# Chunk 5's LayerNorm statistics behind the last kv visit, and the last pair's second product in two column halves

## The chip, the core and the metric

One core of a Trainium2 chip runs the whole program. The metric is the device time of one execution in microseconds. The kernel before took 358.76 us as the median of 3 runs (358.67 to 359.09).

## What is computed

With `q`, `k`, `v` of shape 1 x 2048 x 448, the result is the sum of the input and of two branches on its LayerNorm (no scale, no shift):

```python
x = A_q
xn = _layernorm(x, axis=-1)
return x + _A_ref(xn, A_k, A_v, A_shift_k, A_ssm_k, A_ssm_D) + _B_ref(xn, B_w1, B_b1, B_w2)
```

`_A_ref` makes `kv` (a causal four-tap filter of `k` along the sequence, times `v`), convolves each of its 448 channels with a filter as long as the sequence (written in the reference as a product of FFTs), adds `kv * ssm_D`, and multiplies by `xn`. `_B_ref` is `mish(xn @ w1 + b1) @ w2` with a hidden width of 1792.

## The kernel before

**Two streams of work share every engine.** The dense branch goes through 8 chunks of 256 rows. A chunk is 7 pairs, and a pair is two blocks of 128 hidden columns. For each of the 56 pairs, `g1_mm` (line 514) makes the first product in 22 matmuls of 256 columns, `mish` (lines 522, 86, 87) takes the activation on ScalarE, rounds it to `ach` on ScalarE and makes the rest `acl` on VectorE, and two pairs later `g2_mm` (lines 546 to 548) adds the pair to the second product in 12 matmuls of 448 columns. Each float32 factor is the sum of a rounded part and a rest, so each product is three matmuls.

The long convolution is a Fourier transform in steps. `f1_mm` (line 148) makes the first step of the filter (visits "h") and of `kv` (visits "kv"), `f1_fold` (lines 154, 158) folds it on ScalarE and VectorE, and `f1_out` (line 169) writes it to the scratch tensors `Dh` and `Dkv`. Ahead of each of the 8 kv visits, `taps` (lines 191 to 204) makes `kv` on VectorE, with one tap on GpSimd (line 184). Then come 8 octaves: `hv_mm` (line 237) transforms both sides into `pp`, `pq` and `pr`, which are double-bank PSUM tiles, `h_out` (line 250) copies the filter's side to `hs` on ScalarE, `prod` (lines 259 to 266) multiplies on VectorE, and `i1_mm` (line 276) goes back. `i2_mm` (line 330) and `gate` finish it.

**What sets the order.** A loop over 116 slots, two for each pair, issues everything. Numbers at the head of the file say in which slot each step is issued. Each engine then works its own list strictly in that order. `g1_mm` of pair i stands in slot 2i, `mish` of pair i and `g2_mm` of pair i-2 in slot 2i+1. The last two kv visits are in slots 55 and 59, and the first octave's `hv_mm` is in slot 66.

**The statistics of a chunk.** For chunks 3 to 7, `nt_stats` queues five small VectorE steps on a list called `drip` (two of line 408, two of line 411, and one closure with line 414). `dv()` takes the next step off that list; calls of it are spread over the code, and `flush` takes all that is left. The last step also issues the power -0.5 on GpSimd (line 417) and, on GpSimd's queue, the store of mean and rstd to the scratch tensor `MR` (line 444). `nt_row` (line 447, SyncE's queue) loads one half of `MR` back, broadcast to all partitions, into the columns of `con` called `idr`, a single buffer. `nt_norm` (line 453) applies it to the transposed input `xn` with two VectorE operations. `nt_split` rounds the result to `XH` on ScalarE (line 460) and leaves the rest `XL` on VectorE (line 461). The table `NT_HOW` gives the slots of these steps relative to a base b, which is 56 for chunk 5. Chunk 5's first product starts in slot 70.

**In the first octave** the filter's two halves go to `pp` and `pq`, and the `kv` side's to `pr` and again to `pp`. So the fourth group of matmuls, into `pp`, has to wait until ScalarE's copy `hs<-pp` has read the first.

**The end.** After the last pair (chunk 7, pair 6), `g2_mm` runs for each half of 128 rows, followed by `g2_evac` (line 553, VectorE adds PSUM to `Q`) and a store of 224 KB on SyncE's queue (line 556).

Of the kernel before, what the change touches and what calls it, by code (L numbers as in the profile page):

```python
# [14 lines left out]
S, D, F = 2048, 448, 1792  # L15
NJ = 16
NF = F // 128
NP = NF // 2
CH = 256
NCHUNK = S // CH  # L20
# [13 lines left out]
NT_AT = {"q": -5, "x": -1, "stats": -2, "flush": 0, "row": (4, 8), "norm": (7, 10), "split": (8, 11)}  # L34
NT_SOON = dict(NT_AT, row=(4, 5), norm=(4, 7), split=(6, 8))
NT_HOW = {c: NT_SOON for c in (4, 7)}
NT_HOW[3] = dict(NT_SOON, q=-9, stats=-3, flush=-2)
NT_HOW[5] = dict(NT_AT, q=-8, stats=-4, flush=-2)
EVAC_SOON = 2,
WARM_N = (448, 448, 448)  # L40
FILL_N = (224, 112, 96)
# [3 lines left out]
def tile_kernel(ctx: ExitStack, tc, q, qT, k, v, sk, hT, sD, w10, w1, w2, c_fib, c_g, c_gi, c_i2, out):  # L45
    nc = tc.nc
    V = nc.vector
# [34 lines left out]
    w2h = wp.tile([128, NF, D], F32R, name="w2h")  # L82
    w2l = wp.tile([128, NF, D], F32R, name="w2l")
# [8 lines left out]
    def bank(n):  # L92
        return duo[n // 2][:, n % 2]
# [12 lines left out]
    def dv(n=1):  # L106
        for _ in range(n):
            if drip:
                drip.pop(0)()
# [182 lines left out]
    EE, QA, Q = {}, {}, {}  # L292
# [10 lines left out]
    def late(c):  # L303
        return c >= NCHUNK - LATE
# [84 lines left out]
    def ln_load(c, eng=None):  # L389
        Q[c] = mp.tile([128, 2, D], F32, name="qt", tag="qt", bufs=3)  # L390
        if c:
            nc.sync.dma_start(Q[c], q[:, 2 * c:2 * c + 2])
        else:
            for jj in range(2):
                nc.sync.dma_start(Q[c][:, jj], q[:, jj])
# [4 lines left out]
    def ln_parts(c):  # L400
        st = mp.tile([128, 2, 6], F32, name="bst", bufs=2)
        ve = mp.tile([128, 2], F32, name="ve", bufs=2)
        if c < NT:
            XN[c] = xn = xn_tile().rearrange("p a b -> p (a b)").rearrange("p (j d) -> p j d", j=2)
        eng = nc.gpsimd if 0 < c < NCHUNK - 1 else V

        def stats(jj):
            V.bn_stats(st[:, jj], Q[c][:, jj])

        def aggr(jj):  # L410
            V.bn_aggr(mv[:, 2 * c + jj], st[:, jj])

        def eps(a, b):
            V.tensor_scalar(ve[:, a:b], mv[:, 2 * c + a:2 * c + b, 1], EPS, None, op0=ALU.add)  # L414

        def power(a, b):
            nc.gpsimd.tensor_tensor(rs(c)[:, a:b], ve[:, a:b], mhalf[:, a:b], op=ALU.pow)  # L417

        def norm(jj):
            j = 2 * c + jj  # L420
            eng.tensor_scalar(xn[:, jj, :D], Q[c][:, jj], mv[:, j, 0:1], rs(c)[:, jj:jj + 1],
                              op0=ALU.subtract, op1=ALU.mult)

        def tail(a, b, copy=eng.tensor_copy):
            copy(xn[:, a:b, D:], xn[:, a:b, D - 64:D])

        return stats, aggr, eps, power, norm, tail, ve

    def ln_stats(c):
        stats, aggr, eps, power, norm, tail, ve = ln_parts(c)  # L430
        drip.extend([lambda: stats(0), lambda: stats(1), lambda: aggr(0), lambda: aggr(1), lambda: eps(0, 2),
                     lambda: [f(*a) for f, *a in ((power, 0, 2), (norm, 0), (tail, 0, 1), (norm, 1), (tail, 1, 2))]])
# [47 lines left out]
    def ln_T(c, jj):  # L480
        if jj == 0:
            dv(len(drip))
            x_tiles(c)
        p = pg()
        transposes(c, jj, p)
        for lo in range(2):
            x_split(c, jj, p, lo)


    AHL, P1, P2, GB = {}, {}, {}, {}  # L490
    held, hv = [], set()
    pairs = [(c, p) for c in range(NCHUNK) for p in range(NP)]

    def g1_mm(i):
        c, p = pairs[i]
        XH, XL = XS[c]
        pt = [(bank(GB[i]) if i in GB else pg()).rearrange("p (a b) -> p a b", a=2) for _ in range(2 if i == 0 else 1)]
        ps = [pt[n % len(pt)][:, n] for n in range(2)]
        mm = [[], []]
        for n in range(2):  # L500
            f = 2 * p + n
            fs = slice(128 * f, 128 * f + 128)
            hh, hl, lh = ([(w[:, kt, fs], x[:, kt]) for kt in range(3)] for w, x in ((w1h, XH), (w1h, XL), (w1l, XH)))
            th, tl = ((w1h[:, 3, fs], x[:, 3]) for x in (XH, XL))
            mm[n] = [(n, *m) for m in hh + lh + [th] + hl + [tl]]

            if 0 < i < NP:
                mm[n] = [(n, *m) for m in hh + hl + lh + [th, tl]]
        if i == 0:
            seq = mm[0][:7] + mm[1][:3] + mm[0][7:] + mm[1][7:10] + mm[1][3:7] + mm[1][10:]  # L510
        else:
            seq = mm[0] + mm[1]
        for n_, (n, l, r) in enumerate(seq):
            nc.tensor.matmul(ps[n], l, r, start=all(m[0] != n for m in seq[:n_]), stop=all(m[0] != n for m in seq[n_ + 1:]))  # L514
        P1[i] = ps

    def mish(i):
        p = pairs[i][1]
        ps = P1.pop(i)
        a = mp.tile([128, 2, CH], F32, name="a", bufs=2)  # L520
        for n in range(2):
            nc.scalar.activation(a[:, n], ps[n], AF.Mish, bias=b1t[:, 2 * p + n:2 * p + n + 1])  # L522
            if i == n == 0:
                w1_hi(2)
        if i == 0:
            w1_lo(2)
        ah = mp.tile([128, 2, CH], F32R, name="ach", bufs=3)
        al = mp.tile([128, 2, CH], F32R, name="acl", bufs=3)
        AHL[i] = ah, al
        if 2 * i + 1 in hv:  # L530
            held.append(lambda: split(ah, al, a))
        else:
            split(ah, al, a)
            dv()

    def g2_mm(i, jjs=(0, 1)):
        c, p = pairs[i]
        ah, al = AHL[i]
        for n in range(2):
            f = 2 * p + n  # L540
            for jj in jjs:
                if f == 0:
                    P2[c, jj] = g2p.tile([128, 512], F32, name="pg2")
                ps = P2[c, jj][:, :D]
                cs = slice(128 * jj, 128 * jj + 128)
                nc.tensor.matmul(ps, ah[:, n, cs], w2h[:, f], start=f == 0, stop=False)  # L546
                nc.tensor.matmul(ps, ah[:, n, cs], w2l[:, f], start=False, stop=False)  # L547
                nc.tensor.matmul(ps, al[:, n, cs], w2h[:, f], start=False, stop=f == NF - 1)  # L548

    def g2_evac(c, jjs=(0, 1)):  # L550
        x = Q[c]
        for jj in jjs:
            V.tensor_add(x[:, jj], P2.pop((c, jj))[:, :D], x[:, jj])
            dv()
            if late(c):
                nc.sync.dma_start(out[:, 2 * c + jj], x[:, jj])

    def g2_out(c):
        nc.sync.dma_start(out[:, 2 * c:2 * c + 2], Q[c])

    def mlp_slot(s):
        i, half = divmod(s, 2)
        n = len(pairs)
        j = i - G2_LAG
        if half == 0:
            if i < n:
                c, p = pairs[i]
                if c + 1 < NT:
                    if p == 0:
                        ln_load(c + 1)  # L570
                    if p == (3 if c in (0, 2) else 2):
                        ln_stats(c + 1)
                    if c == 0:
                        dv(len(drip))
                    if p == NP - 1:
                        ln_T(c + 1, 1)
                g1_mm(i)
        else:
            if i < n:
                c, p = pairs[i]  # L580
                if p == NP - 2 and c + 1 < NT:
                    ln_T(c + 1, 0)
                if s not in hv:
                    mish(i)
            if 0 <= j < n - 1:
                g2_mm(j)
                if pairs[j][1] == NP - 1 and pairs[j][0] in EVAC_SOON:
                    g2_evac(pairs[j][0])
            elif j == n - 1:
                for jj in range(2):  # L590
                    g2_mm(j, (jj,))
                    g2_evac(pairs[j][0], (jj,))


    ctx.enter_context(tc.manual_schedule())
# [76 lines left out]
    for c in range(NT, NCHUNK):  # L672
        at_ = NT_HOW.get(c, NT_AT)
        b = 2 * NP * (c - 1) + (1 if c < 5 else 0)
# [36 lines left out]
    stats, aggr, eps, power, norm, tail, ve = ln_parts(0)  # L711
# [5 lines left out]
    ps = [g2p.tile([128, 512], F32, name="pg2") for _ in range(2)]  # L717
# [29 lines left out]
    for s in range(nslots):  # L747
        j = s // 2 - G2_LAG - 1
        if s % 2 == 0 and j >= 0 and pairs[j][1] == NP - 1 and pairs[j][0] not in EVAC_SOON:
            g2_evac(pairs[j][0])  # L750
        if s in hv:
            mish(s // 2)
        for fn, args in plan.pop(s, ()):
            fn(*args)
        mlp_slot(s)
        fns = plan2.pop(s, ())
        for fn, args in fns:
            if fn is i1_out:
                fn(*args)
        for fn, args in fns:  # L760
            if fn is not i1_out:
                fn(*args)
# [69 lines left out]
```

## Time and profile before

| What | Value |
|---|---|
| Median of 3 runs | 358.76 us |
| Span of the profiled execution | 357.0 us (first to last instruction) |
| TensorE busy | 351.0 us, 98% |
| VectorE busy | 270.6 us, 76% |
| ScalarE busy | 156.6 us, 44% |
| GpSimd busy | 70.3 us, 20% |
| Mean granted TensorE clock | 0.998 |

The profiled execution has its span alone; its whole device time isn't listed. The median of the runs is 1.7 us longer than that span, and this stands for what lies around the span. Times in the rows are microseconds from the first instruction. PE is TensorE, PEld its weight loads, DVE VectorE, ACT ScalarE, POOL GpSimd and SP SyncE. In a row of the timeline the first number is the start, the second the duration (a merged row covers several instructions), and the brackets hold the engine's idle time before it and who ended that.

### The profile page before, as it was taken

To read this page: it belongs to the slowest core of one execution; us is meant where nothing else is said; L and a number is where in the kernel's file an instruction comes from. 1 tells how busy PE (TensorE), PEld (TensorE's weight loads), DVE (VectorE), ACT (ScalarE), POOL (GpSimd) and SP (SyncE) were. 2 spreads that over 40 slices of the span, in tenths; PEclk is the share of its full clock that TensorE was granted. 3 is DMA by queue.
4 is the path that set the end of the run, shared out by engine and by line. 5 is a ranking of instruction groups with operands and counts; after the bars stand their busy time and mean duration, and the time that the engine had idled before them with its cause. 6 is when DMAs were issued, how large, how long until landed. Compare 5 with 4: busy or idle time off the path is not lost.

```text
span 357.0 us, 7437 instructions
## 1 busy us (share of the span) xinstructions
PE 351.0 (98%) x3092; PEld 289.5 (81%) x3092; DVE 270.6 (76%) x375; ACT 156.6 (44%) x267; POOL 70.3 (20%) x78
## 2 busy tenths in 40 slices
PE   8999999999999999999999999999999999999995
PEld 2988888888888989888988757666775699979794
DVE  5989748999999999999437756756963933788941
ACT  4966552344243343343233454445445443354470
POOL 2037002822220240212000031011031116040030
PEclk9999999999999999999999999999999999999999
DMA  7998976949768637665869569999896387989086
GB/s 260 344 364 307 411 287 175 340 123 263 198 171 313 164 107 168 223 162 118 245 201 355 201 165 292 248 278 312 276 273 121 77 234 272 409 319 274 19 116 141
DMA packets 30691, 83.27 MB, mean 233 GB/s; under 512 B 3137, under 2 KB 15810, under 8 KB 30658
## 3 DMA queue, kind: packets, MB, share of 16 engines
q1 hardware_dynamic: 21842, 47.82, 39.4%
q0 software_dynamic: 4928, 22.95, 22.9%
q10 hardware_dynamic: 3888, 12.03, 12.8%
q8 instruction: 24, 0.39, 0.4%
q14 instruction: 9, 0.07, 0.1%
HBM read 54.34 MB, written 28.45 MB: 232 GB/s over the span
## 4 chain that ended last, share of the span: by engine, by line
PE 52%; issue 8%; DVE 6%; POOL 2%; DMA 1%
PE pq L514 7%; PE pg L546 7%; PE pg L548 7%; PE pg L547 6%; PE pp L514 5%; PE pr L514 4%; PE pp L237 3%; PE pr L237 3%; PE pp L276 2%; PE pg L514 2%; DVE x L201 2%; POOL x L184 2%; PE pq L237 2%; DMA xn<-in_qT_dram 1%; PE pr L276 1%
## 5 line engine op out<-in xcount | busy, mean ns | idle before, releaser
L546 PE MATMUL pg<-w2h,ach 128*128 128x448 f32 x224 | 82.5, 368 | 0.0
L548 PE MATMUL pg<-w2h,acl 128*128 128x448 f32 x224 | 81.4, 363 | 0.0
L547 PE MATMUL pg<-w2l,ach 128*128 128x448 f32 x224 | 81.2, 362 | 0.0
L87 DVE TENSOR_TENSOR acl<-a,ach 128x512 fp32r<-128x512 f32 x56 | 38.9, 695 | 31.7 <-ACT ach L86 31.5
L522 ACT ACTIVATE a<-pg,b1t 128x256 f32<-128x256 f32 x66 | 27.8, 472 | 65.4 <-PE pg L514 43.3
L514 PE MATMUL pg<-XH,w1h 128*128 128x256 f32 x264 | 52.6, 283 | 0.0
L546 PEld LDWEIGHTS pg<-w2h,ach 128*128 128x128 f32 x224 | 41.9, 187 | 11.5 <-issue 7.2
L514 PEld LDWEIGHTS pg<-XH,w1h 128*128 128x128 f32 x264 | 41.4, 188 | 6.9 <-issue 5.6
L547 PEld LDWEIGHTS pg<-w2l,ach 128*128 128x128 f32 x224 | 42.1, 188 | 2.4
L548 PEld LDWEIGHTS pg<-w2h,acl 128*128 128x128 f32 x224 | 42.1, 188 | 2.4
L514 PE MATMUL pg<-XL,w1h 128*128 128x256 f32 x264 | 42.9, 277 | 0.0
L158 DVE TENSOR_TENSOR st<-pq,st 128x896 f32<-128x896 f32 x32 | 34.8, 1089 | 4.8 <-ACT st L154 4.3
L514 PEld LDWEIGHTS pg<-XL,w1h 128*128 128x128 f32 x264 | 35.9, 188 | 0.0
L86 ACT CAST ach<-a 128x512 fp32r<-128x512 f32 x56 | 34.8, 622 | 1.7
L514 PE MATMUL pg<-XH,w1l 128*128 128x256 f32 x198 | 33.6, 278 | 0.0
L184 POOL TENSOR_TENSOR x<-kr,skb 128x896 f32<-128x896 f32 x8 | 17.0, 2123 | 70.9 <-PE pr L148 26.2
L514 PEld LDWEIGHTS pg<-XH,w1l 128*128 128x128 f32 x198 | 27.6, 188 | 0.2 <-DVE w1l L372 0.2
L201 DVE TENSOR_TENSOR x<-x 128x896 f32<-128x896 f32 x24 | 26.2, 1091 | 1.5 <-POOL x L184 0.8
L522 ACT ACTIVATE a<-pq,b1t 128x256 f32<-128x256 f32 x20 | 8.4, 471 | 31.8 <-PE pq L514 31.8
L287 POOL DMA_DIRECT2D E<-qe x14 | 8.7, 628 | 63.1 <-ACT qe L284 63.1
L154 ACT COPY st<-pr 128x896 f32<-128x896 f32 x16 | 14.5, 908 | 14.2 <-PE pr L148 12.3
L417 POOL TENSOR_TENSOR mv<-ve,mhalf 128x2 f32<-128x2 f32 x5 | 5.0, 1007 | 72.0 <-DVE ve L414 72.0
(138 smaller groups left out, 605.7 us busy)
## 6 DMA issues: line engine op xcount, KB each, us to landing
Dkv<-st ACTq DMA_DIRECT2D x16, 448.0 KB, 5.3
ah<-Dh SPq DMA_DIRECT2D x8, 896.0 KB, 7.5
av<-Dkv SPq DMA_DIRECT2D x8, 896.0 KB, 8.6
e<-E POOLq DMA_DIRECT2D x8, 896.0 KB, 7.2
E<-qe POOLq DMA_DIRECT2D x14, 448.0 KB, 5.9
kr<-in_k_dram SPq DMA_DIRECT2D x10, 448.0 KB, 6.8
Dh<-st ACTq DMA_DIRECT2D x10, 448.0 KB, 6.2
x<-in_hT_dram SPq DMA_DIRECT2D x8, 448.0 KB, 6.0
```

The source lines that it names most:

```text
L86: nc.scalar.copy(h, raw)
L87: V.tensor_sub(l, raw, h)
L154: nc.scalar.copy(st[:, 1], o)
L158: f(st[:, n], e, st[:, 1])
L184: nc.gpsimd.tensor_mul(o, KR[g - u // 2], skb[:, u:u + 1].to_broadcast([128, 2, D]))
L201: V.tensor_add(KV[g], KV[g], o)
L237: nc.tensor.matmul(p[32 * t:32 * t + 32, r, :D], g[rs, t, c], a[rs, t], start=True, stop=True, tile_position=(64 * r, 32 * t))
L514: nc.tensor.matmul(ps[n], l, r, start=all(m[0] != n for m in seq[:n_]), stop=all(m[0] != n for m in seq[n_ + 1:]))
L522: nc.scalar.activation(a[:, n], ps[n], AF.Mish, bias=b1t[:, 2 * p + n:2 * p + n + 1])
L546: nc.tensor.matmul(ps, ah[:, n, cs], w2h[:, f], start=f == 0, stop=False)
L547: nc.tensor.matmul(ps, ah[:, n, cs], w2l[:, f], start=False, stop=False)
L548: nc.tensor.matmul(ps, al[:, n, cs], w2h[:, f], start=False, stop=f == NF - 1)
```

## The change

**First part: chunk 5's statistics.** Its line of `NT_HOW` changes. With b = 56, the load of the chunk's rows moves from slot 48 to 51, the statistics from slot 52 to 61, the flush from 54 to 62, the two `nt_row` from 60 and 64 to 63 and 66, the two `nt_norm` from 63 and 66 to 65 and 66, and the two `nt_split` from 64 and 67 to 65 and 67. So the statistics stand behind the last kv visit (slot 59) instead of ahead of it.

**Second part: the end.** `g2_end` takes the place of the last loop. The second half's sum over the first six pairs is closed early (`stop` at f = 11) and added to `Q` on VectorE while TensorE is at the last pair. The last pair's first half is as before. Its second half is computed in two parts of 224 columns, 6 matmuls each, into one bank of `pp` and one of `pq`. Each part is added by itself and stored by itself, the first on ScalarE's queue, the second on SyncE's.

```diff
-NT_HOW[5] = dict(NT_AT, q=-8, stats=-4, flush=-2)
+NT_HOW[5] = dict(NT_AT, q=-5, stats=5, flush=6, row=(7, 10), norm=(9, 10), split=(9, 11))
...
-                nc.tensor.matmul(ps, al[:, n, cs], w2h[:, f], start=False, stop=f == NF - 1)
+                nc.tensor.matmul(ps, al[:, n, cs], w2h[:, f], start=False, stop=f == NF - 1 or (f == NF - 3 and jj == 1 and c == NCHUNK - 1))
...
+    def g2_end(j):
+        c, p = pairs[j]
+        x, h = Q[c][:, 1], D // 2
+        ah, al = AHL[j]
+        V.tensor_add(x, P2.pop((c, 1))[:, :D], x)
+        g2_mm(j, (0,))
+        g2_evac(c, (0,))
+        for b, cs, eng in ((0, slice(0, h), nc.scalar), (2, slice(h, D), nc.sync)):
+            ps = bank(b)[:, :h]
+            mm = [(a[:, n, 128:], w[:, 2 * p + n, cs]) for n in range(2) for a, w in ((ah, w2h), (ah, w2l), (al, w2h))]
+            for n, (a, w) in enumerate(mm):
+                nc.tensor.matmul(ps, a, w, start=n == 0, stop=n == 5)
+            V.tensor_add(x[:, cs], ps, x[:, cs])
+            eng.dma_start(out[:, 2 * c + 1, cs], x[:, cs])
...
             elif j == n - 1:
-                for jj in range(2):
-                    g2_mm(j, (jj,))
-                    g2_evac(pairs[j][0], (jj,))
+                g2_end(j)
```

**Where instructions move.** The first place is VectorE's list ahead of the last two kv visits. The rows are one piece of the difference (minus is before, plus is after); `bst` and `mv` are the statistics of chunk 5, and lines 191 to 196 are taps of the last kv visit.

```order
 L461 TENSOR_TENSOR XL<-xn,XH 128x4x128
 L87 TENSOR_TENSOR acl<-a,ach 128x512
-L408 BN_STATS bst<-qt 128x6
-L191 TENSOR_TENSOR x<-kr,skb 128x896
-L408 BN_STATS bst<-qt 128x6
-L411 BN_AGGR mv<-bst 128x2 x2
-L414 TENSOR_SCALAR ve<-mv 128x2
+L191 TENSOR_TENSOR x<-kr,skb 128x896
 L194 TENSOR_TENSOR x<-kr,skb 128x448
 L196 TENSOR_TENSOR x<-kr,skb 128x448
```

Five VectorE instructions have left the stretch in which the last `kv` is made, and the taps move up.

The second place is the same list further on, between the last kv visit and the first octave's products (`ya`, `yc`). This is what stands there after; before, the row with line 453 stood one `acl` earlier and there were no statistics.

```order
L87 TENSOR_TENSOR acl<-a,ach 128x512
L408 BN_STATS bst<-qt 128x6 x2
L411 BN_AGGR mv<-bst 128x2 x2
L414 TENSOR_SCALAR ve<-mv 128x2
L87 TENSOR_TENSOR acl<-a,ach 128x512 x2
L453 TENSOR_TENSOR xn<-xn,con 128x4x128 x2
L461 TENSOR_TENSOR XL<-xn,XH 128x4x128
L259 TENSOR_TENSOR ya<-pr,hs 128x896
```

The statistics, the normalisation and the products now follow one another with two `acl` between them.

The third place is ScalarE's list at the first octave. First before, then after; `pg_2103` and `pg_2100` are the first product of the same pair (32), and the two rows of line 250 are the copies that free `pp` and `pq`.

```order
L86 CAST ach<-a 128x512
L460 CAST XH<-xn 128x4x128
L522 ACTIVATE a<-pg_2103,b1t 128x256 x2
L86 CAST ach<-a 128x512
L250 COPY hs<-pp 128x896
L250 COPY hs<-pq 128x896
```

```order
L86 CAST ach<-a 128x512
L522 ACTIVATE a<-pg_2100,b1t 128x256 x2
L86 CAST ach<-a 128x512
L460 CAST XH<-xn 128x4x128
L250 COPY hs<-pp 128x896
L250 COPY hs<-pq 128x896
```

The cast of chunk 5's first half, which follows the normalisation, has moved from ahead of pair 32's activation to directly ahead of the copy that frees `pp`.

## Prediction, on record before the changed kernel ran

> **What bounds the kernel now.** I read the page's busy times first, then who TensorE (PE) waited for, then the timeline of the two places that the change touches.
>
> ```profile
> PE 351.0 (98%) x3092; PEld 289.5 (81%) x3092; DVE 270.6 (76%) x375; ACT 156.6 (44%) x267; POOL 70.3 (20%) x78
> PE pg L696 <- DVE wz L692: 1.0, 1, 1.0
> PE pq L148 <- DVE x L204: 0.7, 1, 0.7
> PE pg L723 <- DVE ve L414: 0.2, 1, 0.2
> ```
>
> PE sets the time. Of its waits only one lies behind the start-up: the last kv visit waits 0.7 us for VectorE's last tap (line 204). So there is little to win: that wait, and what follows the last matmul. A new PE wait costs its full length, since no later one absorbs it. The timeline shows the wait, and the statistics that stand ahead of it on VectorE:
>
> ```profile
> 155.60 0.68 DVE L87 TENSOR_TENSOR acl<-a,ach 128x512 fp32r<-128x512 f32 x1
> 156.21 0.62 DVE L408 BATCH_NORM_STATS2 bst<-qt 128x6 f32<-128x448 f32 x1
> 156.74 1.07 DVE L191 TENSOR_TENSOR x<-kr,skb 128x896 f32<-128x896 f32 x1
> 157.73 0.62 DVE L408 BATCH_NORM_STATS2 bst<-qt 128x6 f32<-128x448 f32 x1
> 158.68 0.62 DVE L194 TENSOR_TENSOR x<-kr,skb 128x448 f32<-128x448 f32 x1
> 167.13 1.09 DVE L204 TENSOR_TENSOR x<-x 128x896 f32<-128x896 f32 x1
> 168.28 0.59 PE L148 MATMUL pq<-x,con 32*64 32x448 f32 x2 [0.66 <-DVE x L204]
> ```
>
> **First part, what goes.** Without the statistics VectorE reaches the taps sooner by 156.74 - 156.21 = 0.53 and 158.68 - 157.73 = 0.95, together 1.48 us. The last tap would end 1.48 earlier, and PE needs it only 0.66 earlier. So the wait goes whole: **-0.66 us**, with 0.8 us to spare. Moving the load of the chunk's rows by three slots past a `v` load on SyncE costs nothing: it is used ten slots later.
>
> **First part, what comes.** The chain statistics, power, store to `MR`, load back, normalisation, cast starts later by nine slots, and ScalarE's cast `XH` now stands directly ahead of the copy `hs<-pp`. Queued behind the cast are both `hs` copies; the octave's second group into `pp` waits for the first copy. I follow the chain with these rows (the three rows of a DMA list give its time to landing, in order for the statistics' store, chunk 5's second `con` load and its first one):
>
> ```profile
> 175.97 0.69 DVE L87 TENSOR_TENSOR acl<-a,ach 128x512 fp32r<-128x512 f32 x1 [2.35 <-ACT ach L86]
> 160.18 0.77 POOL L444 DMA_DIRECT2D MR<-mv  x1 [0.29 <-POOL mv L417]
> MR<-mv POOLq DMA_DIRECT2D x1, 2.0 KB, 3.3
> con<-MR SPq DMA_DIRECT2D x1, 128.0 KB, 4.1
> con<-MR SPq DMA_DIRECT2D x1, 128.0 KB, 6.8
> 185.78 0.69 DVE L87 TENSOR_TENSOR acl<-a,ach 128x512 fp32r<-128x512 f32 x1 [1.50 <-ACT ach L86]
> 181.48 1.41 DVE L453 TENSOR_TENSOR xn<-xn,con 128x512 f32<-128x512 f32 x2
> 182.92 0.62 ACT L460 CAST XH<-xn 128x512 fp32r<-128x512 f32 x1 [2.08 <-DVE xn L453]
> 151.19 0.62 ACT L460 CAST XH<-xn 128x512 fp32r<-128x512 f32 x1 [2.92 <-DVE xn L453]
> 151.72 0.83 ACT L522 ACTIVATE a<-pg,b1t 128x256 f32<-128x256 f32 x2
> 187.69 0.91 ACT L250 COPY hs<-pp 128x896 f32<-128x896 f32 x1 [1.95 <-PE pp L237]
> 188.83 0.96 PE L237 MATMUL pp<-av,g 64*32 64x448 f32 x16
> 182.92 0.32 SPq L447 DMA_DIRECT2D con<-MR  x1
> 195.22 1.41 DVE L453 TENSOR_TENSOR xn<-xn,con 128x512 f32<-128x512 f32 x2
> ```
>
> All times now shift by -0.66. The `acl` of pair 30 starts at 175.97 - 0.66 = 175.31, and the next VectorE instruction follows an `acl` by 156.21 - 155.60 = 0.61: statistics at 175.92. From there to the issue of the store it was 160.18 - 156.21 = 3.97, of which the tap in between took 157.73 - 156.74 = 0.99: so 2.98, issue at 178.90. It lands 3.3 later, at 182.20. SyncE, which waits for this, then issues the load of `con`, and I take 4.1 for it (the load that was issued at about this time before, also behind an `av` load): 186.30. VectorE would be free at 185.78 - 0.66 + 0.61 = 185.73, so it waits 0.6 for the load and starts to normalise at 186.35. The cast follows by 182.92 - 181.48 = 1.44, at 187.79; the `hs` copy by 151.72 - 151.19 = 0.53, at 188.32; it takes 0.91, so with 0.04 for the hand-over PE starts the second `pp` group at 189.27. Without the wait it would be at 188.83 - 0.66 = 188.17. The new wait is **+1.10 us**, more than the old one.
>
> Its bounds: had the load landed in time, VectorE's own end at 185.73 still gives 188.65, a wait of 0.48. With 6.8 for the load, as chunk 5's first one took behind a load of `ah`, it is 191.97, a wait of 3.80. I take the near row since the traffic ahead of it is the same kind. Behind this load on SyncE stand the loads for the coming octaves. Before, they stood behind the second `con` load, issued at 182.92, so an issue at 182.20 holds none of them up. VectorE's products start behind the cast's rest `XL`, but they too wait for `hs`. The second half's normalisation stands behind the products in both kernels (at 195.22 before). Its load can go when the first half is normalised, at about 187.8, so the products hide 7 us of it and I cost it at nothing. A slower one would first hold up the `acl` of pair 33 behind it, which PE uses in slot 69, and from there on cost what it is late.
>
> **Second part.** The early addition to `Q` runs while VectorE idles (it idled 3.50 us before the row at 351.93 below): nothing. The rows of the end, and those that bound a matmul of 224 columns:
>
> ```profile
> 350.53 0.36 PE L546 MATMUL pg<-w2h,ach 128*128 128x448 f32 x1
> 351.93 0.62 DVE L553 TENSOR_TENSOR qt<-pg,qt 128x448 f32<-128x448 f32 x1 [3.50 <-PE pg L548]
> 352.73 0.37 PE L548 MATMUL pg<-w2h,acl 128*128 128x448 f32 x1
> 353.14 0.62 DVE L553 TENSOR_TENSOR qt<-pg,qt 128x448 f32<-128x448 f32 x1 [0.58 <-PE pg L548]
> out_dram<-qt SPq DMA_DIRECT2D x1, 224.0 KB, 1.9
> 171.90 2.51 PE pg L514 x22
> L723 PE MATMUL pg<-wz,ve 128*1 128x224 f32 x2 | 0.5, 352 | 0.0
> 4.87 0.54 PE L723 MATMUL pg<-wz,ve 128*1 128x224 f32 x2
> L514 PE MATMUL pg<-XL,w1h 128*128 128x256 f32 x264 | 42.9, 277 | 0.0
> 170.33 2.22 DVE L158 TENSOR_TENSOR st<-pq,st 128x896 f32<-128x896 f32 x2 [0.47 <-ACT st L154]
> ```
>
> Twelve matmuls of 448 columns start within 352.73 - 350.53 = 2.20, one each 0.200. Those of 256 columns take 2.51 / 22 = 0.114. A matmul of 224 costs 0.100 if time goes by columns, 0.114 if weight loads set a floor; I take 0.114, the nearest row. The narrow ones begin behind six wide ones, at 350.53 + 6 x 0.200 = 351.73, so the last of the twelve starts at 351.73 + 11 x 0.114 = 352.98 instead of 352.73: PE loses 0.25. It lasts 0.27 instead of 0.37 (277 ns for 256 columns), so VectorE starts at 353.29. Its addition costs 0.62 for 448 columns and 1.11 for 896 (half of 2.22), so 0.62 - 0.24 = 0.38 for 224. It ends at 353.67, against 353.76 before: -0.09. The last store has 112 KB instead of 224, which took 1.9: between 0 and -0.9 if all of it went by bytes; I take -0.15, near to none. The first narrow part ends some 0.7 earlier and its store, on ScalarE's free queue, is hidden by the last one. Together **-0.24 us**, between -1.1 and +0.1.
>
> The Trainium skill, "TensorE: Matmul & The Clock Gate", section "LDWEIGHTS (loading the stationary operand)", gives a weight load as columns over 1.2 in ns, so by an estimate from that page 128 columns take 107 ns and the narrow matmuls can't go below it; with that the end would be 0.08 sooner than I say. No row here is narrow enough to show that floor.
>
> [...]
>
> **The sum.** -0.66 + 1.10 - 0.24 = +0.20 on a span of 357.0. The runs' median is 358.76, and I carry the difference over: **358.96 us**. The likeliest case's own range is 358.3 (load in time) to 360.2 (load 1.2 slower than taken). About 0.2% (0.72 us) is what a measurement of this kernel can tell from no change.
>
> **Rivals.**
>
> The gain stays (the cast doesn't hold the copy): -0.66 - 0.24 = -0.90, 357.9. For it: PE had no other wait. Against it: even with the load in time the chain behind pair 32's `acl` makes a wait of 0.48. Chance 7%.
>
> A slow load, slower than before: the load of `con` goes behind the 896 KB of `av`, and lands like the one of 6.8. It decides once store and load together take 0.5 us more than the 7.4 that I assume; at 3.3 + 6.8 the sum is -0.66 + 3.80 - 0.24 = +2.90, 361.7. For it: that row is of the same chunk. Against it: two other rows are near 4. Chance 12%.
>
> Narrow matmuls at the price of plain float32, slower too: the 224-column row at line 723 is a plain float32 matmul in two records; two records of 352 ns within 0.54 start 0.19 apart, so 0.37 for one. Then the last starts at 351.73 + 11 x 0.37 = 355.80 and the end is 2.8 later: -0.66 + 1.10 - 0.24 + 2.8 = +3.0, 361.8. It decides where the narrow matmul exceeds 0.16. Against it: the rounded type goes at the same price per column at 256 and 448. Chance 8%.
>
> **How the numbers follow.** 73% remain for the forecast: 2% of it end faster by over 0.2%, 53% within, 18% slower (load at 4.7 or more). With the rivals: faster 7 + 2 = 9%, within 0.2% 53%, slower 18 + 12 + 8 = 38%. The range 358.1 to 361.2 leaves out the first rival, most of the third and the tail of the second, some 20%.
>
> **What would show it.** Right: no wait at line 148 near 167.6; in the first octave a wait of PE at `pp` for ScalarE's `hs` of about 1 us, with VectorE's line 453 ended by the load of `con`. Wrong: `pp` starts without a gap (first rival), `con` lands later than 187.5 (second), line 569 paced at 0.37 (third), or a PE wait elsewhere.

## The result, and the profile after

| | before | after |
|---|---|---|
| Median of 6 runs each, side by side | 359.02 us (358.67 to 359.31) | 363.22 us (361.46 to 364.84) |
| Ratio | | 1.0117, interval 1.0097 to 1.0137 |
| Span of the profiled execution | 357.0 us | 359.7 us |
| Mean granted TensorE clock in it | 0.998 | 1.000 |

The changed kernel is slower by 4.2 us; 358.96 was predicted, with a range up to 361.2. The profiled execution of the changed kernel is the quickest of its six runs (361.46) and the only one at a granted clock of 1.0; the other five have 0.990 to 0.995 and take 362.84 to 364.84. So two things have to be explained: 2.7 us in a span at full clock, and some 1.8 us more (363.22 - 361.46) in the runs that the trace of that execution doesn't show.

Read first whom TensorE waited for in the changed kernel, behind the start-up:

```profile
PE pp L237 <- ACT hs L250: 3.3, 1, 3.3
```

The wait at line 148 for the last tap is gone. In its place stands one wait of 3.3 us in the first octave, for the copy `hs`. The chain of waits names what is behind it, in order of time (start, length, what):

```profile
177.44 0.73 POOL mv L417
178.18 0.28 issue
178.46 4.43 DMA MR<-mv
182.89 0.02 issue
182.91 5.81 DMA con<-MR
...
188.81 0.70 DVE xn L453
...
189.53 0.70 DVE xn L453
...
190.26 0.02 ACT XH L460
190.28 0.50 issue
190.78 0.91 ACT hs L250
191.69 0.04 issue
191.74 0.99 PE pp L237 x16
```

It is the chain that the prediction followed (power, store, load, normalisation, cast, copy, second `pp` group), with nothing else in it. Of its 14.3 us the store takes 4.43 and the load 5.81. The timeline of the changed kernel shows who stands idle meanwhile:

```profile
167.42 0.59 PE L148 MATMUL pq<-x,con 32*64 32x448 f32 x2
187.40 0.99 PE L237 MATMUL pr<-av,g 64*32 64x448 f32 x16
188.81 1.42 DVE L453 TENSOR_TENSOR xn<-xn,con 128x512 f32<-128x512 f32 x2 [3.09 <-DMA con<-MR]
191.74 0.99 PE L237 MATMUL pp<-av,g 64*32 64x448 f32 x16 [3.35 <-ACT hs L250]
195.27 0.36 PE L546 MATMUL pg<-w2h,ach 128*128 128x448 f32 x1
```

Line 148 starts without a wait, at 167.42 against 168.28. The second `pp` group starts at 191.74 against 188.83: 2.91 us late. Whatever follows keeps that distance to the end: a wait of TensorE is not absorbed later. The rows of the end, in the timeline of the changed kernel:

```profile
354.69 0.26 PE L569 MATMUL pp<-w2h,ach 128*128 128x224 f32 x1
...
355.91 0.27 PE L569 MATMUL pq<-w2h,acl 128*128 128x224 f32 x1
356.22 0.39 DVE L570 TENSOR_TENSOR qt<-pq,qt 128x224 f32<-128x224 f32 x1 [0.28 <-PE pq L569]
```

The first narrow matmul starts at 354.69; the prediction had its place before the shifts at 351.73, so the work arrives 2.96 late. The first and the last of the twelve are 1.22 us apart, 0.111 us each. VectorE ends at 356.61, where it ended at 353.76 before: 2.85 late, so the narrow halves win back 0.11. With the spans 2.7 apart the last store, which lands after 1.7 instead of 1.9, gives back about 0.15 more.

### The profile page after: what moved, and what is told of

Same layout as the page of the kernel before. It is cut to its first block, busy times and chain, and to the rows that moved or that the text cites. A ratio compares the mean times of both kernels' runs of the same rounds, so it can differ in the third digit from the quotient of the medians.

```text
span 359.7 us, 7455 instructions
## 1 busy us (share of the span) xinstructions
PE 351.8 (98%) x3098; PEld 290.0 (81%) x3098; DVE 271.5 (75%) x377; ACT 156.5 (44%) x267; POOL 70.0 (19%) x78
## 4 chain that ended last, share of the span: by engine, by line
PE 46%; issue 8%; DMA 3%; POOL 1%; DVE 0%; ACT 0%; DVEq 0%; POOLq 0%
PE pq L514 7%; PE pg L546 6%; PE pg L548 6%; PE pg L547 5%; PE pp L514 5%; PE pr L514 4%; PE pp L237 2%; PE pr L237 2%; PE pp L276 2%; DMA con<-MR 2%; PE pq L237 1%; PE pr L276 1%; DMA MR<-mv 1%; PE pp L330 1%; POOL x L184 1%
```

## The experiments

All times are medians beside runs of the kernel before on the same chip, and the ratios are against those.

**1. The first part alone.** Only the table's line is changed; the end is as before.

```diff
-NT_HOW[5] = dict(NT_AT, q=-8, stats=-4, flush=-2)
+NT_HOW[5] = dict(NT_AT, q=-5, stats=5, flush=6, row=(7, 10), norm=(9, 10), split=(9, 11))
```

> The first part alone (chunk 5's statistics moved, the end as before). Theory A: the whole loss sits in the first octave, where ScalarE's cast XH waits for the late load of con and holds the copy hs that frees pp; in the changed kernel's profile that wait was 3.35 us, and the wait removed 0.66. Without the end's 0.3 us this gives 359.02 - 0.66 + 3.35 = 361.7, and up to 363.6 in executions whose granted clock is below 1, with the same spread of some 2 us. Rival B: the loss and the spread come from the second part (narrow matmuls, the store on ScalarE's queue): then about 358.4 here, without spread.

Measured: 363.74 us (363.16 to 364.19, 4 runs), ratio 1.0131 (1.0117 to 1.0145). The whole loss is in the first part, the lower clock too: all four runs have 0.993 to 0.995.

**2. The second part alone.** The changed kernel with the old line of the table.

```diff
-NT_HOW[5] = dict(NT_AT, q=-5, stats=5, flush=6, row=(7, 10), norm=(9, 10), split=(9, 11))
+NT_HOW[5] = dict(NT_AT, q=-8, stats=-4, flush=-2)
```

> The second part alone (the last pair in two column halves, the statistics as before). Theory A: a gain of 0.3 us, 358.7, with no more spread than before. Rival B (the loss sits in the second part): 361 to 363.

Measured: 358.61 us (358.31 to 358.92, 11 runs), ratio 0.9989 (0.9980 to 0.9998). The new end alone is worth 0.4 us, between 0.1 and 0.7.

**3. The cast behind the copies.** In the changed kernel the first `nt_split` goes one slot later, so ScalarE copies `hs` first and casts afterwards.

```diff
-NT_HOW[5] = dict(NT_AT, q=-5, stats=5, flush=6, row=(7, 10), norm=(9, 10), split=(9, 11))
+NT_HOW[5] = dict(NT_AT, q=-5, stats=5, flush=6, row=(7, 10), norm=(9, 10), split=(10, 11))
```

> As the changed kernel, but the first half's cast and rest (nt_split) one slot later, so that ScalarE's cast XH stands behind the two hs copies; statistics, loads and normalisation stay. Theory A: PE no longer waits at pp, since the copies wait for PE alone: 359.02 - 0.66 - 0.3 = 358.0, with no spread. Rival C: the late load still holds VectorE's products behind the normalisation, and the wait only moves to the product's first user on PE, or the load is slow enough to delay chunk 5's first product: 360 to 361.

Measured: 359.80 us (359.36 to 360.60, 9 runs), ratio 1.0022 (1.0012 to 1.0031). With the cast out of the way the wait at `pp` is gone, and with it 3.4 of the 4.2 us: this placement is what turns a late load into a wait of TensorE. Both forecasts missed (358.0, and 360 to 361). Another wait shows in its place among TensorE's waits:

```profile
PE pr L237 <- DMA av<-Dkv: 0.7, 1, 0.7
```

The `av` load of this octave lands late here. In the changed kernel's own profiled execution it lands barely in time: TensorE's weight loads wait for it, and the `pr` group itself is only 0.08 late (187.40 - 186.57, where it was 188.08 - 187.33 before).

```profile
PEld pr L237 <- DMA av<-Dkv: 0.7, 1, 0.7
```

The next run asks how usual a longer wait is.

**4. The changed kernel again**, unchanged.

> The changed kernel once more, for a second profile. Its six runs went from 361.46 to 364.84, and the granted clock was 1.0 in the fastest and 0.990 to 0.995 in the others. Theory A with the clock: PE waits 3.3 us or more at pp, and when the time is over 362 the granted clock drops in the stretch right behind that wait; the wait itself is of about the same length. Rival D: the clock stays at 1 around the wait and the longer runs have a longer wait (5 us or more), or the drop is in another place.

Measured: 362.90 us in one run, span 361.1, granted clock 0.993. Here are TensorE's groups of the first octave and what follows, from the timeline, and its clock in stretches of 2 us (TensorE busy, weight loads, VectorE, ScalarE, GpSimd, granted clock, DMA share, GB/s):

```profile
188.33 0.99 PE L237 MATMUL pr<-av,g 64*32 64x448 f32 x16 [0.75 <-DMA av<-Dkv]
191.65 1.09 PE L237 MATMUL pp<-av,g 64*32 64x448 f32 x16 [2.33 <-ACT hs L250]
192.67 1.01 PE L514 MATMUL pq<-XH,w1h 128*128 128x256 f32 x3
...
196.75 0.36 PE L546 MATMUL pg<-w2h,ach 128*128 128x448 f32 x1
```

```profile
192.00:194.00 2.00, 2.00 (x22) 1.33 (x7) 2.00 (x3) 0.40 (x1) 0.00 (x0) 0.60 1.06 376
194.00:196.00 2.00, 2.00 (x12) 2.00 (x12) 2.00 (x3) 0.00 (x0) 0.00 (x0) 0.54 1.01 352
```

The wait is in two pieces, 0.75 for `av` and 2.33 for `hs`, and the second `pp` group starts as late as in the first profile (191.65 and 191.74). But behind it the granted clock is 0.60 and 0.54 for about 4 us, and three matmuls of 256 columns take 1.01 instead of 0.62. From the `pp` group to the first row of line 546 it takes 196.75 - 191.65 = 5.10, against 195.27 - 191.74 = 3.53 at full clock: 1.57 us lost without any wait. It accounts for the 1.44 us that this run has over the profiled one; the other five of the six are 1.4 to 3.4 us over it, and they have no trace.

**5. The statistics one slot sooner** in the changed kernel, to give store and load more time.

```diff
-NT_HOW[5] = dict(NT_AT, q=-5, stats=5, flush=6, row=(7, 10), norm=(9, 10), split=(9, 11))
+NT_HOW[5] = dict(NT_AT, q=-5, stats=4, flush=5, row=(7, 10), norm=(9, 10), split=(9, 11))
```

> As the changed kernel, but the statistics one slot earlier (stats=4, flush=5), so that VectorE makes them right behind the last kv visit's fold, some 2.7 us sooner, ahead of pair 30's rest acl; the cast stays ahead of the copies. Theory A: the store is then over before the 896 KB load av starts, con lands at about 184.5, VectorE's own end (185.7) sets the cast, and PE's wait at pp falls to about 0.5 us: 359.0 - 0.7 + 0.5 - 0.3 = 358.5, no drop of the granted clock, no spread. Rival C (the load of con is slow whenever it shares the queues with av): the wait stays above 1.5 us, 359.5 or more.

Measured: 363.79 us (363.08 to 364.05, 4 runs), ratio 1.0131 (1.0117 to 1.0144). Nothing was won. The DMA list and two rows of the timeline say why:

```profile
MR<-mv POOLq DMA_DIRECT2D x1, 2.0 KB, 6.4
con<-MR SPq DMA_DIRECT2D x1, 128.0 KB, 6.6
```

```profile
175.97 0.77 POOL L444 DMA_DIRECT2D MR<-mv  x1 [0.29 <-POOL mv L417]
...
192.17 1.06 PE L237 MATMUL pp<-av,g 64*32 64x448 f32 x16 [3.63 <-ACT hs L250]
```

The store went out 2.5 us sooner, 3.6 us behind the last two writes of `Dkv`, and took 6.4 instead of 4.4; the load took 6.6 instead of 5.8. The writes of `Dkv` themselves land later beside it (5.7 in the changed kernel, 6.7 here, the median of the two). SyncE's `av` load, which waits for them, goes out at 182.08 instead of 179.80, and the load of `con` 0.43 behind it. What goes out sooner doesn't land sooner here.

**6. Both of these**, statistics one slot sooner and the cast behind the copies.

```diff
-NT_HOW[5] = dict(NT_AT, q=-5, stats=5, flush=6, row=(7, 10), norm=(9, 10), split=(9, 11))
+NT_HOW[5] = dict(NT_AT, q=-5, stats=4, flush=5, row=(7, 10), norm=(9, 10), split=(10, 11))
```

> Statistics one slot earlier and the cast behind the copies (split at slot 66). Theory A: no wait at all in the first octave, the whole gain of both parts: 359.0 - 0.7 - 0.3 = 358.0. If the late av load that PE met in the cast-behind-copies run (0.7 us) has another cause than the small store to MR ahead of it, it stays and this gives 358.8 or more.

Measured: 359.58 us (359.32 to 360.19, 11 runs), ratio 1.0018 (1.0009 to 1.0027). The first octave runs without a wait. Then TensorE waits in the second:

```profile
PE pp L237 <- ACT a L522: 0.9, 1, 0.9
```

The second half's normalisation stands behind the products that the first half delayed, its cast behind that, and pair 34's activation behind the cast. So the lateness was passed on and not removed.

**7. The wait filled.** In the changed kernel 20 tiny matmuls on zeros (8 x 64, into columns of `pr` that nobody reads) stand between the first octave's `pr` and second `pp` group.

```diff
-FILL_N = (224, 112, 96)
+FILL_N, FILL = (224, 112, 96), 20
...
-        PS["V", o] = [f2_mm(AV[o], o, c, vb[c]) for c in range(2)]
+        PS["V", o] = [f2_mm(AV[o], o, 0, vb[0])]
+        if o == 0:
+            for n in range(FILL):
+                nc.tensor.matmul(PS["V", o][0][0:8, n % 2, 448:512], wz, wz[:, 0:1].to_broadcast([128, 64]), start=True, stop=True)
+        PS["V", o].append(f2_mm(AV[o], o, 1, vb[1]))
```

> The changed kernel with 20 small matmuls (8 zero weights, 64 columns, into unused columns 448 to 511 of pr) on PE between the first octave's third and fourth group, where it waits for the copy. They compute nothing that is used. Theory A with the clock: they fill some 2 us of the wait without lengthening it, the granted clock stays at 1, and the time falls from 363 to about 361.5 with less spread. Rival D (the longer runs have longer waits, and the clock is a by-product): 363 and the same spread as before.

Measured: 361.68 us (361.45 to 362.61, 5 runs), ratio 1.0076 (1.0062 to 1.0089). In its profiled execution the second `pp` group starts even later than in the changed kernel, and the clock stays whole:

```profile
192.93 0.99 PE L237 MATMUL pp<-av,g 64*32 64x448 f32 x16 [1.19 <-ACT hs L254]
```

```profile
192.00:194.00 2.00, 1.07 (x17) 1.00 1.06 374
194.00:196.00 2.00, 2.00 (x18) 1.00 1.09 363
```

(The columns here are TensorE's busy time, granted clock, DMA share and GB/s.) Its five runs have granted clocks of 0.998 to 1.0, against 0.990 to 0.995 in five of the six of the changed kernel. By the ratios, useless work in the gap makes the kernel 1.5 us quicker (1.0076 for 1.0117): so most of the loss over the profiled execution is the clock, and the idle time sets it off.

**8. Without the store.** The changed kernel without chunk 5's store to `MR`; the rows are loaded from chunk 4's, so chunk 5 is normalised with chunk 4's statistics. The load of `con` waits for no store then.

```diff
+        if c == 5:
+            return
...
-        nc.sync.dma_start(idr, MR[c][jj].partition_broadcast(128))
+        nc.sync.dma_start(idr, MR[4 if c == 5 else c][jj].partition_broadcast(128))
```

> The changed kernel without chunk 5's store to MR; its rows are loaded from chunk 4's MR instead (so chunk 5 is normalised with chunk 4's statistics). Everything else stays in place. Theory S (the 2 KB store in 8-byte pieces slows the av load that is issued during it): av lands in about 5 us as before the change, PE doesn't wait for it, con lands at about 185 and the wait at pp is about 0.5 us: 358.5. Rival L (av is late because it shares the engines with con and the loads behind it): PE still waits 0.6 us or more for av: 359.2 or more.

Measured: 359.84 us (359.29 to 360.30, 11 runs), ratio 1.0023 (1.0015 to 1.0032). Rows of its timeline, and of its DMA list:

```profile
186.85 1.42 DVE L455 TENSOR_TENSOR xn<-xn,con 128x512 f32<-128x512 f32 x2 [0.94 <-DMA con<-MR]
187.51 0.96 PE L237 MATMUL pr<-av,g 64*32 64x448 f32 x16
189.78 0.99 PE L237 MATMUL pp<-av,g 64*32 64x448 f32 x16 [1.31 <-ACT hs L250]
```

```profile
con<-MR SPq DMA_DIRECT2D x1, 128.0 KB, 6.4
```

The wait for `av` is gone. But the load, now issued right behind the `av` load, takes 6.4, and a wait of 1.31 is left. So even without any store the cast ahead of the copy costs more than the tap's 0.66. Both forecasts missed: theory S had `av` right, but `con` at about 185, and it landed at 186.8; the rival's time came without the wait for `av` that it rests on.

The DMA traffic of this stretch bears on the store. Three rows of the windows, 182 to 184 us, for the kernel before, the changed kernel and this one (granted clock, DMA share, GB/s):

```profile
182.00:184.00 2.00, 1.00 0.99 372
```

```profile
182.00:184.00 2.00, 1.00 0.40 57
```

```profile
182.00:184.00 2.00, 1.00 1.03 399
```

Where the `av` load runs at 372 and 399 GB/s, the changed kernel moves 57. Is it the store of 2 KB, in pieces of 8 bytes, that does this? Run 11 asks.

**9. Another way to the same gain.** The second part alone, with the statistics where they were; the last visit's first tap goes from VectorE to GpSimd, where its third one is made already.

```diff
+        if g == NO - 1:
+            after(52, taps_pool, g, 0)
```

> The second part of the change alone, and instead of moving the statistics, the last kv visit's first tap (line 191, 0.99 us on VectorE) is made on GpSimd like its third one; the statistics stay ahead of the visit. Theory A (the wait at the last kv visit is VectorE's lateness of 0.66 us and nothing else, and moving the statistics lost only by what they start later): VectorE is 0.9 us sooner, the wait goes, and nothing new waits: 359.0 - 0.66 - 0.4 = 357.9. Rival: PE gains nothing because another wait (GpSimd's other tap or the power, behind this tap on its queue) takes its place: 358.6, as the second part alone.

Measured: 358.37 us (358.12 to 358.68, 11 runs), ratio 0.9979 (0.9971 to 0.9988). This beats the kernel before by 0.7 us and is the best version of the study. The wait at the last kv visit shrinks from 0.66 to the first row here; the forecast was that it goes:

```profile
PE pq L148 <- DVE x L204: 0.3, 1, 0.3
...
155.81 2.42 POOL L184 TENSOR_TENSOR x<-kr,skb 128x896 f32<-128x896 f32 x1 [7.14 <-DVE x L183]
157.58 0.68 DVE L414 TENSOR_SCALAR ve<-mv 128x2 f32<-128x2 f32 x1
```

The other two rows show a reason. The last step of the statistics, which stays on VectorE, takes 0.68 beside GpSimd's new tap and ends 0.03 behind it; in run 2 it takes 0.17. That is 0.51 of the 0.9 us that VectorE was to gain.

**10. Everything later, two buffers.** The changed kernel with the statistics one slot sooner, normalisation and cast behind the octave's copies, and a buffer of its own for the second half's rows, so that its load needn't wait for the first half.

```diff
-NT_HOW[5] = dict(NT_AT, q=-5, stats=5, flush=6, row=(7, 10), norm=(9, 10), split=(9, 11))
+NT_HOW[5] = dict(NT_AT, q=-5, stats=4, flush=5, row=(7, 8), norm=(10, 10), split=(11, 11))
...
-        nc.sync.dma_start(idr, MR[c][jj].partition_broadcast(128))
+        ID[c, jj] = i = t2([128, CH], "idr2") if c == 5 and jj else idr
+        nc.sync.dma_start(i, MR[c][jj].partition_broadcast(128))
```

> As the changed kernel with the statistics one slot earlier, and the late load taken out of everybody's way: the second half's rows go to a buffer of their own, both halves are loaded together, normalised behind the first octave's products, and cast behind both copies and pair 33's activation. Theory A (only what stands behind the late load waits): PE has no wait at pp, at most 0.3 us at the second octave's pp, 359.0 - 0.66 + 0.3 - 0.4 = 358.2. Rival C (the small store slows what is in flight beside it, so that av or the Dkv writes are late for PE whatever the order): 359 or more.

Measured: 358.68 us (358.42 to 359.40, 11 runs), ratio 0.9991 (0.9982 to 1.0000). The first octave is free of waits, but TensorE then waits for a load of the second:

```profile
PE pr L237 <- DMA ah<-Dh: 0.8, 1, 0.8
```

The time lies between the two forecasts. So moving the statistics, with all that was tried to cover it, comes out 0.3 us better than the kernel before (0 to 0.6), no more than the 0.4 that the second part alone gives.

**11. The store alone.** The second part alone, statistics in their old place, plus a store of the same shape to a scratch that nobody reads or waits for, in the slot where the changed kernel has its own.

```diff
+    spare = dp.tile([2, CH], F32, name="spare")
+
+    def spare_store():
+        t = t2([128, 2, 2], "spare")
+        V.tensor_copy(t, mv[:, 10:12])
+        nc.gpsimd.tensor_tensor(t[:, :, 1], t[:, :, 1], mhalf, op=ALU.pow)
+        nc.gpsimd.dma_start(spare.rearrange("j (p t) -> p j t", t=2), t)
+
+    at(62, spare_store)
```

> The kernel with only the second part of the change (358.61 in its own run), plus one piece of the first part alone: in slot 62 a copy of two small rows on VectorE, a power of them on GpSimd, and a store of 2 KB in pieces of 8 bytes to a scratch that nobody reads. Nothing waits for this store; what it leaves in is only its traffic, issued near 178 us, shortly ahead of the load of 896 KB of av. Theory S, the small store slows the big load beside it: av lands some 3 us later than without, TensorE waits 0.5 to 0.8 us for av at the first group of the first octave, time 359.1 to 359.4. Rival, the store's traffic is harmless and av came late in the changed kernel for another reason: no wait for av, time 358.5 to 358.8.

Measured: 359.02 us (358.53 to 359.46, 11 runs), ratio 0.9998 (0.9989 to 1.0007), and no wait for `av`: as a forecast of the time the theory missed. It is 0.4 us over run 2's median, but the two intervals overlap. What the theory says of the loads shows in the DMA lists. First the second part alone (run 2), then with the store (run 11):

```profile
av<-Dkv SPq DMA_DIRECT2D x1, 896.0 KB, 4.9
...
con<-MR SPq DMA_DIRECT2D x1, 128.0 KB, 4.4
```

```profile
av<-Dkv SPq DMA_DIRECT2D x1, 896.0 KB, 6.2
...
con<-MR SPq DMA_DIRECT2D x1, 128.0 KB, 6.1
...
spare<-spare POOLq DMA_DIRECT2D x1, 2.0 KB, 5.2
```

A store of 2 KB that nobody waits for makes the 896 KB beside it land 1.3 us later, and the 128 KB behind it 1.7 later. Each list is one execution, but the others agree: without a store in that place (before, runs 2, 9 and 12) this `av` load lands after 4.7 to 4.9 and the load of `con` after 4.1 to 4.4. From 182 to 184 us run 2 moves 346 GB/s and run 11 moves 89. In run 11's schedule both loads had that much to spare. In the changed kernel neither has: there the store goes out with 1.3 us between it and the `av` load (178.46 and 179.80), here with 2.2 (178.57 and 180.75), and the load of `con` is what the chain waits for.

**12. The tap one slot sooner**, on run 9, to take the last 0.29 us. The load of the visit's rows of `k` stands one slot sooner too.

```diff
-        at(t - d - (3 if g > 1 else 2), k_load, g)
+        at(51 if g == NO - 1 else t - d - (3 if g > 1 else 2), k_load, g)
...
-            after(52, taps_pool, g, 0)
+            after(51, taps_pool, g, 0)
```

> The kernel with only the second part of the change, the first tap of the last kv visit on GpSimd (358.37 in its run) and that tap asked for one slot sooner. If the 0.29 us of wait that were left at the last kv visit came from VectorE waiting for GpSimd's tap and power, they go: time 358.0 to 358.2. Rival: the tap can't start sooner, since its rows are used by TensorE and VectorE until then, or the wait has another source: time 358.3 to 358.5 and the wait stays near 0.3.

Measured: 359.82 us (359.53 to 361.33, 11 runs), ratio 1.0025 (1.0016 to 1.0034); worse, which neither side had expected. The earlier load isn't the reason: it goes out at 143.4 us in run 9 and here. Rows of GpSimd, VectorE and TensorE in its timeline:

```profile
155.20 2.41 POOL L184 TENSOR_TENSOR x<-kr,skb 128x896 f32<-128x896 f32 x1 [6.54 <-DVE x L183]
155.57 2.60 DVE L87 TENSOR_TENSOR acl<-a,ach 128x512 fp32r<-128x512 f32 x1
...
169.25 0.59 PE L148 MATMUL pq<-x,con 32*64 32x448 f32 x2 [1.70 <-DVE x L204]
```

Begun while GpSimd's tap runs (155.20 to 157.61), VectorE's `acl` takes 2.60 instead of 0.69 and ends 0.56 after the tap, nearly the time that it takes alone. What follows on VectorE is late with it, and the wait at the last kv visit grows from 0.29 to 1.70. In run 9 the tap began 0.24 us behind the `acl`, at 155.81, and the `acl` took its 0.69. The Trainium skill, "SBUF — State Buffer", section "Who interferes with whom", says that a VectorE instruction with two inputs in SBUF and a GpSimd instruction that reads SBUF lock each other out, and that the order of issue decides who is blocked; these two traces agree.

## Why the prediction was wrong, point by point

**The wait at the last kv visit goes, -0.66.** Right. The row at 167.42 has no wait; up to the octave's `pr` group TensorE is 0.68 ahead (187.40 against 188.08).

**A new wait in the first octave, +1.10.** The mechanism was right to the last link; the size was not. In the same terms it is (191.74 - 187.40) - (188.83 - 188.08) = 3.59, so this term alone is 2.5 us short. The step that failed is the time taken for store and load together, by the sentence "I take the near row since the traffic ahead of it is the same kind". The store was taken at 3.3 and took 4.4, the load at 4.1 and took 5.8. Together 10.2 instead of 7.4, less 0.4 because the store went out at 178.46 and not at 178.90. The traffic was not the same kind, since the store itself is part of it: before, it went out 18 us sooner (160.18), and now it goes ahead of the `av` load. Run 11 shows just that: with a store in that slot a load of `con` goes from 4.4 to 6.1. Run 8 shows the other side: without any store, but issued right behind the `av` load, it takes 6.4. That in both it is the `av` load still under way that holds it up is argued, not shown. Why the store itself takes 3.3 in one place and 4.4 in another stays open too. The row that the load's time was taken from has the two loads nearly as far apart as the changed kernel (`av` at 180.21 and `con` at 182.92 there, 179.80 and 182.91 here). What it lacks is the store: there the `av` load landed after 4.7, here TensorE's weight loads waited for it until the `pr` group at 187.40, 7.6 behind its issue.

**The slow load as a rival.** It gave 361.7, decided by store and load together over 7.9, and 12%. This is what came: 10.2, and 361.46 in the execution at full clock. That 3.3 + 6.8 is so near to 10.2 is luck in part, as the store took 1.1 more than that and the load 1.0 less, and the rival didn't have the store slow anything. The range ended at 361.2, so it left out the rival's own figure and not only its tail. Against it I had set that "two other rows are near 4". In this stretch the load took 5.8 in the changed kernel and 6.6 and 6.4 in runs 5 and 8, which moved or removed the store: here the far row (6.8) was the nearer one.

**What the sum didn't have: the clock.** A wait was priced at its length. But the clock falls behind it in most executions, and that costs another 1.6 us (run 4) that no wait shows. Run 7 separates the two. The Trainium skill, "TensorE: Matmul & The Clock Gate", section "HAM oscillation — how this bites in real kernels", says that TensorE must not idle for more than about 3.4 us at a stretch, or its clock is throttled. Two traces agree: 3.35 in one piece left the clock at 1.0, and 3.63 in one piece (run 5) was followed by 0.74 and 0.50. As a limit on one gap it doesn't cover run 4, where 0.75 and 2.33 with 1 us of work between them were followed by 0.60, nor run 1 with 0.57 and 2.35. What decides which executions fall stays open.

**The end, -0.24.** Right within its error: 0.11 up to VectorE's end (0.09 said) and about 0.15 for the store (0.15 said) in the profile, and -0.4 (-0.7 to -0.1) in run 2. The narrow matmuls go at 0.111, not at 0.100 by columns and not at the plain type's 0.37; that rival is refuted. By the Trainium skill, "TensorE: Matmul & The Clock Gate", section "LDWEIGHTS (loading the stationary operand)", the floor was 107 ns by an estimate; the rows' 111 agree within 4 ns.

**"I cost it at nothing", the second half's normalisation.** In the changed kernel itself TensorE has no wait from it. Where only the first octave was freed of its wait it wasn't free: in run 6 exactly this piece, cast and activation behind it, cost 0.9.

**The sum.** In the profile: -0.68 + 3.59 = 2.91 at the second `pp` group, 2.96 at the first narrow matmul, and 0.11 + 0.15 less at the end: 2.7, which is the difference of the spans. For the median the clock adds about 1.8.

## What to carry to other kernels

A step that stores and loads back through DRAM brings traffic with it, so when it is moved, its own store belongs to the traffic of the place it is moved to: price it and its neighbours as slowed by each other, and not by rows in which each ran alone. A short cast put ahead of the copy that frees a PSUM buffer puts the whole chain behind the cast on the path of TensorE; look what the engine's list makes wait for the moved instruction. And a TensorE wait of some 3 us can cost half as much again through the clock, which shows in the spread of the runs and in the granted clock, not in the waits.

## What the runs showed of the hardware that was not expected

- After about 3 us of idle time within 4 us (2.92, 3.08 and 3.63), the granted clock fell to about half for some 4 us in three profiled executions (0.67 and 0.50 in run 1, 0.60 and 0.54 in run 4, 0.74 and 0.50 in run 5, in the two stretches from 192 to 196 us), and did not in the first profile of the changed kernel (3.35). With tiny matmuls on zeros in the gap (run 7) it stayed at 1.0.
- A store of 2 KB in pieces of 8 bytes made a load of 896 KB land after 6.2 us instead of 4.9, and one of 128 KB after 6.1 instead of 4.4 (runs 11 and 2). Such a store itself took 3.3 us before, 4.4 in the changed kernel, 5.2 in run 11, 6.4 in run 5 and 7.0 in run 10. That the pieces of 8 bytes are the reason wasn't tried.
- A VectorE operation of 0.69 us took 2.60 when it began during a GpSimd tap, and 0.69 when it began 0.24 us ahead of it. One of 0.17 us took 0.68 and ended 0.03 behind the tap (run 9).
